# Half-width pairs for the first sixteen expert blocks of the output products

## The chip, the core and the metric

One core of a Trainium2 chip runs the whole kernel. It has five engines that run side by side: TensorE (matmuls, in the profile PE, and its weight loads, PEld), VectorE (DVE), ScalarE (ACT), GpSimd (POOL) and SyncE (SP), which issues most of the DMAs. TensorE reads two operands from the on-chip memory: a stationary one, which a weight load puts into the array of 128 rows and 128 columns, and a moving one, whose columns are streamed through it. It writes sums into eight accumulator banks of 128 partitions by 512 single-precision numbers.

The metric is device time in microseconds (us), the median of the runs.

## The reference

Input `x` has 2048 tokens of D = 576 numbers. Two results are mixed by a gate g, a sigmoid of a weighted sum of the token:

```
g = sigmoid((x * gate_w).sum(-1))
a = long convolution of x with a kernel K (a state space model), plus x * Dskip
b = expert layer:
    q = x @ w_q                  # 32 heads, two halves of 128 each
    s1, s2 = q1 @ k1.T, q2 @ k2.T    # 64 scores each
    the best two of s1 and of s2 give 4 candidates, the best two of them are kept
    weights = softmax of these two
    b = sum over heads and kept experts of  weight * gelu(x . u[e]) * v[e]
out = g * a + (1 - g) * b
```

There are 64 x 64 = 4096 experts, so `u` and `v` are 4096 x 576.

## The kernel before

The tokens are worked on in 16 tiles of 128. The kernel computes `x . u[e]` for all 4096 experts (tiles `a`), the scores (`s`), the convolution by matmuls with Fourier tables (`kb`, `kP`, `u`, `k`, `pr`, `pi`, `pv`, `y`), and then, tile by tile, a dense matrix of 128 tokens by 4096 experts that holds the weights at the kept experts and zeros elsewhere, multiplied by gelu of `x . u[e]`. The output stage multiplies this matrix with `v`.

For a token tile, the weighted matrix is made in `prep` (L1498): one-hot matrices `A`, `Bg` on VectorE, `S` on TensorE (L1528, four bursts of 32 matmuls, two banks each), the product with gelu (`gl`) on VectorE, and the split of the result into two 16-bit parts `wh` (L1558): `h[0]` the value rounded to 16 bits, `h[1]` what is left. Each has 32 blocks of 128 experts (partitions) by 128 tokens. `v` lies split in the same way in `vhl`, eight tiles of four blocks.

The output loop (L1775 to L1805) goes over the tiles in the order of `ORDER` (0, 15, 1, 14, ...). For each tile it takes two banks `po[0]` and `po[1]`, one for each half of D (288 columns). For each of the 32 blocks it issues three products (high by high, high by low, low by high) for both halves: six matmuls with the stationary operand `h[wz][:, b, :]` (128 experts by 128 tokens) and the moving operand 288 columns of `vhl`. A tile is 192 matmuls. The last tile in the order goes through one half of D after the other (L1793 to L1802), so that the first half can be finished while the second is summed up. `finish` (L1632) adds the result to `ya`, which holds the gated convolution from `y_part` (L1566), and sends it out.

What stands between these matmuls on TensorE is decided when the program is built. `mm` (L207) adds an estimated duration to a clock, and `pump` (L220) is called after each block and runs every waiting piece of work (a generator) that is due by that clock: a burst of `S` for the next tile, or the `y` matmuls of the next two tiles. `mm` also counts a change in the shape of the array's use with 0.13 or 0.1 us. The engines then run what was issued in that order, and wait only where data or a bank is not there yet.

Some matmuls use only a part of the array: `wb` (L593) and `tr` put 64 columns on each half of the array's columns, `kb` and `y` 32 columns on each quarter, `u` 64 rows on each half of the rows, `pr` and `pv` quadrants. Single-precision matmuls appear in the profile as two instructions each.

The helper `mm` records every matmul, so all of them have line L214; the tiles' names tell them apart.

Of the kernel before, what the change touches and what calls it, by code (L numbers as in the profile page):

```python
# [138 lines left out]
def body(ctx: ExitStack, tc: tile.TileContext, xT, au, par, logdt, dskip, gatew, wq, kT, uT, vv,  # L139
# [17 lines left out]
    def key(x):  # L157
        n = x.tensor.name
        return (n, x.offset) if n in columns else n

    def size(x):
        n = 1
        for d in x.shape[1:]:
            n *= d
        return n
# [41 lines left out]
    def mm(o, l, r, start, stop, cost=None):  # L207
        m = l.shape[0] > 64, 128 if size(l) > 64 else size(l)
        if m != tiling[0]:
            tiling[0] = m  # L210
            clock[0] += 0.13 if m == (True, 128) else 0.1
        clock[0] += (size(r) * (4 if r.dtype == F32 else 1) / 2400 + 0.003) if cost is None else cost
        rdy[key(o)] = clock[0] + 0.4
        T.matmul(o, l, r, start=start, stop=stop)  # L214

    def spawn(gen, after=0.0):
        heapq.heappush(heap, (clock[0] + after, nseq[0], gen))
        nseq[0] += 1

    def pump():  # L220
        while heap and heap[0][0] <= clock[0]:
            _, _, gen = heapq.heappop(heap)
            try:
                spawn(gen, next(gen) or 0.0)
            except StopIteration:
                pass
# [8 lines left out]
    def ready(*xs, late=0.0):  # L235
        while True:
            t = max(rdy.get(key(x), 0.0) for x in xs) + late - clock[0]
            if t <= 0:
                return
            yield t  # L240

    def wait(gen):
        for t in gen:
            idle(t)
# [16 lines left out]
    def need(tag, n=1):  # L261
        while True:
            lst = sorted(slots[tag])
            if len(lst) >= n and lst[n - 1] <= clock[0]:
                return
            yield max(0.2, lst[n - 1] - clock[0]) if len(lst) >= n else 0.3
# [6 lines left out]
    def free(tag, *outs):  # L273
        if owed[tag]:
            owed[tag] -= 1
            return
        slots[tag].append(max([clock[0]] + [rdy.get(key(x), 0.0) for x in outs]))
# [12 lines left out]
    def bank(tag, name):  # L290
        take(tag, name)
        t = ps.tile([128, 512], F32, tag="ps", name=name, bufs=8)
        banks.add(t.tensor.name)
        return t
# [1326 lines left out]
    def finish_half(t, po, hh):  # L1621
        yield from ready(po[hh])
        a = yt[t]
        half_rows(t, a, po, hh)
        yield from ready(a)
        cs = slice(288 * hh, 288 * hh + 288)
        for n, (d, o) in enumerate(au_rows(out, t, a)):
            dma(d[:, cs], o[:, cs], nc.scalar if hh and n % 2 else None)
        if hh:
            finished[t] = 1  # L1630

    def finish(t, po):  # L1632
        yield from ready(*po)
        while t not in yt:
            yield 0.3
        a = yt.pop(t)
        for hh in range(2):
            half_rows(t, a, po, hh)
        yield from ready(a)
        for d, o in au_rows(out, t, a):  # L1640
            dma(d, o)
        finished[t] = 1
# [54 lines left out]
    def until(f, dt=0.3):  # L1697
        while not f():
            idle(dt)
# [10 lines left out]
    for w, n in ((0, 9), (1, 5)):  # L1710
        for xk in [x for k in range(4) for x in (k, 4 + k)[:2 - w]] + [8]:
# [3 lines left out]
            for j in range(4):  # L1715
                cs = slice(128 * j, 128 * j + 128)
# [58 lines left out]
    for t in ORDER:  # L1775
        until(lambda: t in st)
        h = st.pop(t)
        wait(ready(*h))
        wait(need("sc", 2))
        po = [bank("sc", f"o{t}_{hh}") for hh in range(2)]  # L1780
        for b in range(32):
            if t == ORDER[0] and b % 4 == 0:
                until(lambda: len(vhl) > b // 4)
                wait(ready(vhl[b // 4]))
            if t == ORDER[-1]:
                break
            vc = vhl[b // 4]
            for n, (wz, vz) in enumerate(((0, 0), (0, 1), (1, 0))):
                for hh in range(2):
                    mm(po[hh][:, :288], h[wz][:, b, :], vc[:, b % 4, vz, 288 * hh:288 * hh + 288],  # L1790
                       b == 0 and n == 0, b == 31 and n == 2)
            pump()
        if t == ORDER[-1]:  # L1793
            until(lambda: t in yt)
            for hh in range(2):
                for b in range(32):
                    for n, (wz, vz) in enumerate(((0, 0), (0, 1), (1, 0))):
                        mm(po[hh][:, :288], h[wz][:, b, :], vhl[b // 4][:, b % 4, vz, 288 * hh:288 * hh + 288],
                           b == 0 and n == 0, b == 31 and n == 2)
                    pump()  # L1800
                spawn(finish_half(t, po, hh))
            break  # L1802
        free("slot")
        free("slot")
        spawn(finish(t, po))  # L1805
# [42 lines left out]
```

## Time and profile before

| what | value |
|---|---|
| median of three runs | 1449.73 us (1449.56 to 1449.82) |
| span of the profiled execution | 1447.6 us |
| `o` matmuls, busy, count | 387.0 us, 3072 |
| `s` and `a` matmuls, busy | 363.9 and 359.7 us, 1536 each |
| `S` matmuls, busy, count | 72.3 us, 2048 |
| `y` matmuls, busy, count | 17.2 us, 256 |
| weight loads of `wh`, busy, count | 296.0 us, 3072 |
| output stage on TensorE, first to last `o` start | 995.8 to 1443.7 us |

The span is the time from the first to the last instruction of one profiled execution. Busy time of an engine is the time in which at least one of its instructions runs; the ends of matmuls are modelled, so one `o` matmul is shown with 286 ns though another starts before it has ended. Durations below are therefore taken from start to start. A row of the timeline has the start, the time up to the last end of the row, the engine, the operation with output and inputs, the shapes, and the number of instructions.

### The profile page before, as it was taken

What the parts mean: (1) busy time and instruction counts of PE and PEld (TensorE: products, weight loads), DVE (VectorE), ACT (ScalarE), POOL (GpSimd) and SP (SyncE); (2) the same over time, 40 slices, a digit from 0 to 9 for tenths busy, and PEclk for the clock granted to TensorE, in tenths of its full rate; (3) what the DMA queues carried; (4) which work ended last, traced back from release to release, by engine and by line L of the source; (5) the groups of instructions that cost most, each with busy time, mean ns of one, the idle gap of its engine ahead of it and who ended that gap; (6) DMA issues with size and microseconds to landing.
All of it is one profiled execution on the core that took longest, in us unless ns stands there. A gap on an engine that the chain in (4) does not pass through costs nothing.

```text
span 1447.6 us, 36680 instructions
## 1 busy us (share of the span) xinstructions
PE 1426.9 (99%) x14105; PEld 852.3 (59%) x14105; DVE 1208.5 (83%) x4598; ACT 769.6 (53%) x1285; POOL 481.5 (33%) x491
## 2 busy tenths in 40 slices
PE   7999999999999999999999999999999999999998
PEld 3444445455455445445555444456887887888787
DVE  6899899889877997885899897589999988888850
ACT  6346876796684776844656655655434223323310
POOL 0325357547356436220547899600000000000000
PEclk9999999999999999999999999999999999999999
DMA  8235323342324333169675777776543333342400
GB/s 308 74 117 159 96 74 120 125 143 72 117 93 150 95 105 99 49 199 293 209 272 179 255 256 270 267 259 210 196 127 111 108 120 107 123 145 68 157 10 17
DMA packets 134351, 215.42 MB, mean 149 GB/s; under 512 B 10912, under 2 KB 79904, under 8 KB 127776
## 3 DMA queue, kind: packets, MB, share of 16 engines
q1 hardware_dynamic: 134080, 213.01, 45.5%
q8 instruction: 110, 1.80, 0.5%
q14 instruction: 65, 0.53, 0.1%
q10 hardware_dynamic: 96, 0.07, 0.0%
HBM read 141.74 MB, written 71.30 MB: 147 GB/s over the span
## 4 chain that ended last, share of the span: by engine, by line
PE 89%; DMA 2%; DVE 2%; issue 0%; ACT 0%; SPq 0%; ACTq 0%; DVEq 0%
PE o L214 26%; PE s L214 24%; PE a L214 23%; PE S L214 4%; PE kb L214 2%; PE pr L214 2%; PE wb L214 2%; PE y L214 1%; PE kP L214 1%; PE pv L214 1%; PE u L214 1%; PE k L214 1%; DMA z_d<-vo 1%; DMA ksb<-k_d 1%; DVE i L134 1%; DMA vn<-in_au_dram 0%
## 5 line engine op out<-in xcount | busy, mean ns | idle before, releaser
L214 PE MATMUL o<-vhl,wh 128*128 128x288 f16 x3072 | 387.0, 286 | 0.0
L214 PE MATMUL s<-whl,xb 128*128 128x512 f16 x1536 | 363.9, 379 | 0.0
L214 PE MATMUL a<-xb,uhl 128*128 128x512 f16 x1536 | 359.7, 379 | 0.2 <-DVE go L134 0.2
L214 PEld LDWEIGHTS <-wh 128*128 128x128 f16 x3072 | 296.0, 98 | 76.3 <-issue 3.7
L214 PEld LDWEIGHTS <-xb 128*128 128x128 f16 x1792 | 170.6, 98 | 210.1 <-issue 15.3
L214 PEld LDWEIGHTS <-uhl 128*128 128x128 f16 x1536 | 147.3, 98 | 176.2 <-issue 3.4
L134 DVE FIND_INDEX8 i<-m,s 128x8 uint32<-128x64 f32 x1024 | 206.5, 222 | 0.0
L134 ACT ACTIVATE wh<-gl,s_wg 128x1024 f16<-128x1024 f32 x64 | 68.9, 1137 | 202.3 <-DVE gl L134 202.3
L134 DVE MAX8 m<-s 128x8 f32<-128x64 f32 x1024 | 146.3, 215 | 29.3 <-PE s L214 28.4
L134 POOL TENSOR_TENSOR CS<-CS,ex 128x512 f32<-128x512 f32 x72 | 98.0, 1393 | 147.6 <-DVE ex L134 146.2
L134 ACT ACTIVATE go<-a,i_a 128x512 f32<-128x512 f32 x94 | 63.2, 685 | 96.4 <-PE a L214 68.6
L134 DVE TENSOR_TENSOR gl<-S,gl 128x256 f32<-128x256 f32 x256 | 90.5, 416 | 12.6 <-PE S L214 8.3
L134 POOL TENSOR_TENSOR e<-aN,rt 128x512 f32<-128x512 f32 x72 | 83.2, 1177 | 49.9 <-PE kb L214 43.7
L134 DVE SCALAR_TENSOR_TENSOR wh<-gl,s_wg,wh 128x1024 f16<-128x1024 f32 x63 | 78.6, 1280 | 10.7 <-ACT wh L134 10.7
L134 DVE TENSOR_TENSOR Bg<-Be,vals 128x1024 f16<-128x1024 f16 x128 | 84.6, 702 | 2.2
L134 ACT ACTIVATE gl<-gl 128x1024 f32<-128x1024 f32 x64 | 63.5, 1045 | 34.2 <-DMA gl<-g_d 31.1
L134 DVE TENSOR_TENSOR A<-iota_a,vals 128x2048 f16<-128x2048 f16 x64 | 77.9, 1216 | 0.0
L214 PE MATMUL s<-wrem,xb 128*128 128x512 f16 x256 | 76.2, 379 | 0.0
L214 PE MATMUL a<-xb,wrem 128*128 128x512 f16 x256 | 75.9, 379 | 0.0
L214 PEld LDWEIGHTS <-A 128*128 128x128 f16 x2048 | 70.5, 97 | 4.7
L134 DVE MATCH_VALUE_LOAD i<-m,s 128x8 f32 x1024 | 72.6, 71 | 0.1
L214 PE MATMUL S<-Bg,A 128*128 128x64 f16 x2048 | 72.3, 193 | 0.0
(205 smaller groups left out, 2068.5 us busy)
## 6 DMA issues: line engine op xcount, KB each, us to landing
g_d<-go SPq DMA_DIRECT2D x128, 256.0 KB, 2.5
gl<-g_d SPq DMA_DIRECT2D x32, 1024.0 KB, 5.4
wq<-in_wq_dram SPq DMA_DIRECT2D x16, 1152.0 KB, 6.0
su_d<-us SPq DMA_DIRECT2D x32, 288.0 KB, 2.6
sk_d<-k1o SPq DMA_DIRECT2D x32, 288.0 KB, 2.9
ui<-su_d SPq DMA_DIRECT2D x16, 576.0 KB, 4.0
ki<-sk_d SPq DMA_DIRECT2D x16, 576.0 KB, 5.3
vn<-in_vv_dram SPq DMA_DIRECT2D x32, 288.0 KB, 5.4
```

The source lines that it names most:

```text
L134: return f(*a, **k)
L214: T.matmul(o, l, r, start=start, stop=stop)
```

## The change

In the output loop, for all tiles but the last of the order, the blocks 0 to 15 are computed with half the tokens at a time. For each of the six former matmuls there are two: the tokens 0 to 63 (m = 0) on the array's first 64 columns and the tokens 64 to 127 (m = 1) on its last 64. The two that follow one another work on different halves of D, and so on different banks and different moving operands: with `hh = 0`, m = 0 goes to `po[0]` and m = 1 to `po[1]`; with `hh = 1` the other way round. Over both values of `hh` each quarter of the output (64 tokens by 288 columns) gets the same three products as before. The first product of block 0 opens the sum in each of the four quarters; the blocks 16 to 31 go on adding in the full shape. The planner's duration of one such matmul is given as 0.061 us.

```diff
             for n, (wz, vz) in enumerate(((0, 0), (0, 1), (1, 0))):
                 for hh in range(2):
+                    if b < 16:
+                        for m in range(2):
+                            cs = slice(64 * m, 64 * m + 64)
+                            z = 288 * (hh ^ m)
+                            mm(po[hh ^ m][cs, :288], h[wz][:, b, cs], vc[:, b % 4, vz, z:z + 288],
+                               b == 0 and n == 0, False, 0.061)
+                        continue
                     mm(po[hh][:, :288], h[wz][:, b, :], vc[:, b % 4, vz, 288 * hh:288 * hh + 288],
-                       b == 0 and n == 0, b == 31 and n == 2)
+                       False, b == 31 and n == 2)
             pump()
```

## The prediction

> **What bounds the kernel now.** I read the head of the page first, then the chain that ended last, then the output stage alone.
>
> ```profile
> span 1447.6 us, 36680 instructions
> ...
> PE 1426.9 (99%) x14105; PEld 852.3 (59%) x14105; DVE 1208.5 (83%) x4598; ACT 769.6 (53%) x1285; POOL 481.5 (33%) x491
> ...
> PEclk9999999999999999999999999999999999999999
> ...
> PE 89%; DMA 2%; DVE 2%; issue 0%; ACT 0%; SPq 0%; ACTq 0%; DVEq 0%
> PE o L214 26%; PE s L214 24%; PE a L214 23%; PE S L214 4%; PE kb L214 2%; PE pr L214 2%; PE wb L214 2%; PE y L214 1%; PE kP L214 1%; PE pv L214 1%; PE u L214 1%; PE k L214 1%; DMA z_d<-vo 1%; DMA ksb<-k_d 1%; DVE i L134 1%; DMA vn<-in_au_dram 0%
> ```
>
> TensorE is busy 99% of the span at full granted clock, and 89% of the chain is its work; the largest piece, 26%, is `o`, the products that the change rewrites. A busy TensorE need not be at its peak, so the next views are of the output stage: busy time of each engine in 50 us of it, then who waited for whom from 1000 us on (total us, times, longest).
>
> ```profile
> 1150.00:1200.00 50.00, 50.00 (x608) 41.18 (x610) 42.87 (x74) 15.10 (x15) 0.00 (x0) 1.00 0.39 124
> ```
>
> ```profile
> DVE ya L134 <- PE o L214: 58.0, 14, 20.2
> ...
> DVE gl L134 <- PE S L214: 7.7, 9, 1.6
> ...
> PEld L214 <- issue: 3.7, 8, 0.5
> ```
>
> The columns are PE, PEld, DVE, ACT, POOL, granted clock, DMA share and GB/s. TensorE has no idle time. VectorE is busy 42.87 of 50 us and waits for TensorE (58.0 and 7.7 us), not the other way round; the weight loads never wait longer than 0.5 us. So a nanosecond added to TensorE here is a nanosecond added to the end, and there is no wait in which it could vanish.
>
> The timeline of TensorE over one output tile and its neighbours (start us, us to the modelled end, what, how many) gives the rates, from start to start:
>
> ```profile
> 1163.01 15.60 PE L214 MATMUL o<-vhl,wh 128*128 128x288 f16 x126
> 1178.45 1.13 PE L214 MATMUL S<-Bg,A 128*128 128x64 f16 x32
> 1179.42 0.90 PE L214 MATMUL o<-vhl,wh 128*128 128x288 f16 x6
> 1180.15 1.13 PE L214 MATMUL S<-Bg,A 128*128 128x64 f16 x32
> 1181.12 4.57 PE L214 MATMUL o<-vhl,wh 128*128 128x288 f16 x36
> 1185.53 1.13 PE L214 MATMUL S<-Bg,A 128*128 128x64 f16 x32
> 1186.50 3.84 PE L214 MATMUL o<-vhl,wh 128*128 128x288 f16 x30
> 1190.17 1.13 PE L214 MATMUL S<-Bg,A 128*128 128x64 f16 x32
> 1191.14 8.25 PE L214 MATMUL o<-vhl,wh 128*128 128x288 f16 x66
> 1199.32 2.15 PE L214 MATMUL y<-yz,tf 128*32 128x288 f32 x32
> 1201.40 0.30 PE L214 MATMUL o<-vhl,wh 128*128 128x288 f16 x1
> ```
>
> 126 `o` take 1178.45 - 1163.01 = 15.44 us, 122.5 ns each. The bursts of `S`, 32 matmuls in 0.97 us, cost nothing extra at their edges: 30 `o` from 1186.50 to 1190.17 are 3.67 us, 122.3 ns each. Before `y`, which runs in another shape (four groups of 32 columns), it is different: 66 x 0.1225 = 8.09 us, but `y` starts after 8.18, so 0.09 us are lost at the change of shape.
>
> **The change part by part.** *Removed:* in 15 tiles, 16 blocks x 3 products x 2 halves of D = 96 full matmuls each, 1440 in all. *Added:* 2880 matmuls of 64 tokens, in 1440 pairs, with 2880 weight loads of 64 columns in place of 1440 of 128. Nothing else is moved by hand: same operands, same banks, same end of each sum, no DMA and no wait added. Each pair streams 288 columns on both halves of the array, so the question is what a pair costs, and what the added changes of shape cost.
>
> *The pair.* No row shows a 16-bit pair of 288 columns on two column halves. The nearest rows: `u`, 16-bit pairs on two row halves; `y` above, four column groups with four different moving operands; and the 64-column loads and matmuls of `tr`.
>
> ```profile
> 97.69 0.91 PE L214 MATMUL u<-uh,tu 64*128 64x288 f16 x12
> 98.54 0.60 PE L214 MATMUL s<-wrem,xb 128*128 128x512 f16 x2
> ...
> 933.82 0.20 PEld L214 LDWEIGHTS <-vals 128*64 128x64 bf16 x4
> ...
> 933.88 0.26 PE L214 MATMUL tr<-identb,vals 128*64 128x64 bf16 x4
> ```
>
> 12 `u` take 98.54 - 97.69 = 0.85 us, 6 pairs of 0.126 after 0.09 for the change of shape: two row halves run side by side at the price of one full matmul. For `y`, from the first start to the last (2.15 less the 0.41 of one matmul) seven groups of four take 1.74 us, 0.249 a group, or 0.124 for every two matmuls of 288 columns, with four operands read at once in a wider type. So two halves of the array reading two operands are not beyond the reading side. If four column groups run two by two, or as one at half speed, a pair of `o` comes out at 0.1225 either way. Bounds: 0.1225 (no row of 288 columns is shorter) and the 0.126 of `u`, 1440 x 3.5 ns = 5.0 us. I take 0.1225, a pair at the price of the full matmul, since both rows still hold a first load that nothing hides.
>
> *The loads.* A `tr` load of 64 columns starts 0.06 us before its first matmul (933.82 to 933.88): that is what it costs where nothing hides it. Within a run of pairs it lies beside 0.1225 us of the pair before, as 0.059 a pair does even where the matmuls are short (`wb`, below). Cost 0; if that cover were gone, 1440 x 0.06 = 86 us, but `wb` and `y` show loads and matmuls of the same groups overlapped. The Trainium skill, "TensorEngine Tiling (Array Packing)", section "Feature Incompatibilities", speaks against the change: column tiling is mutually exclusive with the fast weight load; by its "TensorE: Matmul & The Clock Gate", section "LDWEIGHTS (loading the stationary operand)", 64 columns then take 64/1.2 = 53 ns, an estimate. The trace agrees (0.06 us), and by the page the sum would be the same, since 53 ns is shorter than a pair.
>
> *The issue.* Four instructions in 122.5 ns instead of two. In `kb` the engine takes them faster:
>
> ```profile
> 164.89 0.32 PE L214 MATMUL kb<-Y,CS 128*32 128x64 f32 x8
> ...
> 166.59 0.29 PE L214 MATMUL kb<-e,CS 128*32 128x64 f32 x8
> ```
>
> 16 such rows of 8, from 164.89 to 166.88 (the last start plus its 0.29), are 128 matmuls in under 2 us, 16 ns each with its load, where the change asks for one in 61. Cost 0.
>
> *The change of shape.* `wb` has the very shape of the change, 128 rows by 64 columns:
>
> ```profile
> 24.27 0.81 PE L214 MATMUL a<-xb,uhl 128*128 128x512 f16 x3
> 25.01 2.32 PE L214 MATMUL wb<-kt,wq 128*64 128x64 f32 x72
> 27.26 2.76 PE L214 MATMUL a<-xb,uhl 128*128 128x512 f16 x12
> 29.86 0.38 PE L214 MATMUL a<-xb,wrem 128*128 128x512 f16 x1
> ```
>
> An `a` takes (29.86 - 27.26)/12 = 0.217 us, three 0.65, and `wb` starts after 0.74: 0.09 to drain on the way in, as before `y`. 72 `wb` last 2.25 us to the next `a`; from first to last start they take 2.32 - 0.22 = 2.10, 0.059 for each of 36 pairs, 2.11 in all: 0.14 us remain, of which 0.05 is the first load that nothing hides and 0.09 to 0.10 the drain on the way out. With 0.02 for the first full load and the skew of the last pair (an estimate: the rows are read to 0.01), one visit to the half-column shape costs 0.255 us. Bounds: 0.19 (two drains of 0.095, loads hidden) and 0.30 (a load of 0.06 exposed on both sides).
>
> *How many visits.* Each of 15 tiles enters the shape at block 0 and leaves it after block 15: 15 visits. `S` stays in the full shape, so each burst of `S` inside the first sixteen blocks adds one. I cut the 15 stretches of 96 `o` out of the trace and counted the `S` in each (us, PE busy and count, DVE, clock, DMA):
>
> ```profile
> 1023.45:1039.27 15.82, 2.26 (x64) 3.78 (x11) 1.00 0.44 153
> 1053.99:1066.66 12.67, 1.13 (x32) 2.83 (x8) 1.00 0.55 161
> 1082.35:1097.19 14.84, 1.13 (x32) 1.82 (x6) 1.00 0.09 22
> 1111.92:1125.55 13.63, 2.26 (x64) 1.41 (x4) 1.00 0.82 254
> ...
> 1367.15:1382.97 15.82, 2.26 (x64) 1.41 (x4) 1.00 0.27 86
> 1396.72:1408.42 11.70, 0.00 (x0) 0.00 (x0) 1.00 0.11 25
> ```
>
> Ten stretches in a row, 1111.92 to 1382.97, have 64 (two bursts); before them 64, 32, 32; the first and the last stretch none. A burst is 32, so 20 + 4 = 24. `y` lies inside seven first halves; it changes the shape on both sides before and after, so it adds no visit, only the exposed 64-column load on the way back, 7 x 0.04 = 0.3 us. In the first tile `y` stands where block 15 ends and saves half a visit, 0.13.
>
> *The sum.* (15 + 24) x 0.255 = 9.9, + 0.3 - 0.1 = 10.1 us, all of it on TensorE and on the path. The span goes from 1447.6 to 1457.7; the median lies 2.1 us above the span (1449.73 - 1447.6), so **1459.8 us**, 0.7% slower. The cost model of the planner counts a change of shape with 0.1 and 0.13, so later `S` bursts move back against the blocks by a block or so; the two in a first half stand at blocks 12 to 14, those of the second half from 19 on, and only in the third and fourth tile do some stand at 16 to 18. I allow 22 to 30 bursts. What waits behind a drain is only the next matmul; VectorE gets its `S` later by at most one drain and has 7 of 50 us to spare. The last tile (237 `o` from 1414.74, no change of shape) is not touched.
>
> ```profile
> 1414.74 29.20 PE L214 MATMUL o<-vhl,wh 128*128 128x288 f16 x237
> ```
>
> **Rivals.** *A, the pair costs a few ns more than a full matmul* (its two starts are not hidden): 1.44 us for each ns; at 7 ns 1459.8 + 10.1 = 1470. Against it: `u` at 0.126 with its first load in it. 13%.
>
> *B, the change does not do what it says: the halves run only partly side by side, or one after the other.* One after the other, 1440 x 0.1225 = 176 us more: 1636. Against it: 32 `y` of 288 columns take 2.08 us, where 32 x 0.1225 = 3.92 would be the least in series. Partly: if four fifths of the overlap come, a pair takes 0.1225/0.79 = 0.155, 47 us more: 1507. The Trainium skill, "TensorE: Matmul & The Clock Gate", section "Measured speedup vs the span model", has three column tiles at 2.38 times one, which is this 0.79; the trace speaks against it, as groups of `y` come at twice 0.124. 3% together.
>
> *C, not slower: a pair streams faster than a full matmul.* Place: the 1440 pairs; each ns under 122.5 gives 1.44 us back, and at 122.5 - 10.1/1.44 = 115.5 ns the drains are paid for: 1449.7. Below that the kernel would be faster. For it: nothing in a run of `o` shows whether the last 2 ns are the array or the hand-over between matmuls; against it: no row of 288 columns comes under 0.122. 3%, of which 1% is faster.
>
> *D, the order of the bursts shifts.* If none of the `S` fell into a first half, 24 visits fewer: 1459.8 - 6.1 = 1453.7; if all four did in 14 tiles, 71 visits, 32 more: 1468.0. 8%, mostly between.
>
> **How the numbers follow.** Forecast 73%, its own bounds 37 x 0.19 = 7.0 and 45 x 0.30 = 13.5, so 1456.7 to 1463.2. For 8 in 10 I add the nearer part of A (up to 5 ns, 7.2 us: 1467) and of D: **1455.5 to 1467**. A measurement can tell about 0.2%, 2.9 us, from no change: for that fewer than 12 visits would have to be paid, and the tiles alone make 15. Faster 1%, within 0.2% 2%, slower 97%.
>
> **What would show it.** In the profile after: pairs of `o` with 64 columns at 122.5 ns from pair to pair (A and B: longer, C: shorter); 0.09 us lost before and after each run of them, and a first pair about 0.05 late; 22 to 30 bursts of `S` inside first halves; still no idle TensorE and the same granted clock; other stages unchanged. I am wrong if TensorE's gaps at the edges are under 0.05 us, if pairs are not at 122.5, or if a weight load becomes what the matmuls wait for.

## The result and the profile after

| | before | after |
|---|---|---|
| median, us | 1449.82 (1449.56 to 1452.7, 5 runs) | 1460.03 (1456.4 to 1460.77, 5 runs) |
| span of the profiled execution, us | 1447.6 | 1458.8 |
| first to last start of an output matmul, us | 447.9 | 456.8 |

The ratio is 1.0061, with a 95% interval of 1.0043 to 1.0078: slower by 0.6%, at 1460.0 us where 1459.8 was forecast, in the range of 1455.5 to 1467. Two more sets of runs say the same: 1.0064 (1.0047 to 1.0081) for the changed kernel again, 1.0004 (0.9993 to 1.0016) for the kernel before against itself.

The last row of the table is read from these two, before and after: count, then shortest, median and longest duration in ns, then the first and the last start in us (the counts behind the shapes are of a sample). With one more digit of the trace the differences are 1443.65 - 995.77 = 447.9 and 1454.89 - 998.09 = 456.8.

```profile
L214 PE MATMUL o<-vhl,wh x3072: 283/286/297, 995.8 to 1443.7; 128*128 128x288 f16 x192
```

```profile
L214 PE MATMUL o<-vhl,wh x4512: 283/286/310, 998.1 to 1454.9; 128*64 128x288 f16 x124, 128*128 128x288 f16 x73
```

The head of the page after:

```profile
span 1458.8 us, 39560 instructions
...
PE 1436.8 (98%) x15545; PEld 871.6 (60%) x15545; DVE 1210.2 (83%) x4598; ACT 770.2 (53%) x1285; POOL 481.5 (33%) x491
```

1440 more matmuls and as many loads, as counted, and about 10 us more of TensorE's time. VectorE has the same instructions as before. Whether TensorE waits now is read from the view of who waited for whom, from 998 us on:

```profile
DVE ya L134 <- PE o L214: 62.8, 15, 20.4
...
PEld L214 <- issue: 14.2, 54, 0.5
DVE gl L134 <- PE S L214: 11.2, 9, 1.8
```

The order of who waits has not changed: VectorE for TensorE, a little longer than before (58.0 and 7.7 us then). The one row that grew for TensorE is the weight loads' (3.7 us in 8 waits, now 14.2 in 54): by their places in the trace, the 8 are the returns from `y`, and the 46 new ones all stand at a change into or out of the half-column shape.

Where the time lies shows in the timeline of TensorE, here over the paired blocks of one tile. `128*128` is the full shape, `128*64` the half columns; two of the latter are a pair. The row of `o` between the first two that are shown is left out, as it holds matmuls of both shapes, and the last row ends where the view does.

```profile
1138.07 1.13 PE L214 MATMUL S<-Bg,A 128*128 128x64 f16 x32
...
1147.33 2.15 PE L214 MATMUL y<-yz,tf 128*32 128x288 f32 x32
1149.41 6.07 PE L214 MATMUL o<-vhl,wh 128*64 128x288 f16 x96
1155.41 1.14 PE L214 MATMUL S<-Bg,A 128*128 128x64 f16 x32
1156.48 1.66 PE L214 MATMUL o<-vhl,wh 128*64 128x288 f16 x24
1158.07 1.14 PE L214 MATMUL S<-Bg,A 128*128 128x64 f16 x32
1159.14 1.05 PE L214 MATMUL o<-vhl,wh 128*64 128x288 f16 x14
```

A "drain" is here, as in the prediction, the time lost between the last matmul of one shape and the first of another; what TensorE does in it, no run shows. 96 half matmuls, 48 pairs, take 1155.41 - 1149.41 = 6.00 us; 48 x 0.1225 is 5.88, and 0.12 remain for one late first pair and one drain. 24 of them take 1.59 us, 12 x 0.1225 = 1.47 and again 0.12. And a burst of `S` that stood free of cost among full matmuls (0.97 us) now takes 1.07 us to the next pair (1155.41 to 1156.48): the other drain, 0.10. So the time is at the edges, 0.22 us for each visit to the half-column shape, and none in the pairs.

Taken over all starts of the stage, pairs follow one another every 122 or 123 ns (1346 intervals, without the first of each run of pairs), as full matmuls do, and the terms of a visit are these: into the shape 0.092 to 0.093 us, a first pair of 0.1465 instead of 0.1225 (0.024), out of it 0.099, and about 0.01 for the first full matmul after it, 0.224 together. There are 40 visits, 15 for the tiles and 25 for bursts of `S`: 9.0 us, of 456.8 - 447.9 = 8.9.

### The profile page after: what moved, and what is told of

It is laid out like the page before. It is cut to its first block, busy times and chain, and to the rows that moved or that the text cites. A ratio compares the mean times of both kernels' runs of the same rounds, so it can differ in the third digit from the quotient of the medians.

```text
span 1458.8 us, 39560 instructions
## 1 busy us (share of the span) xinstructions
PE 1436.8 (98%) x15545; PEld 871.6 (60%) x15545; DVE 1210.2 (83%) x4598; ACT 770.2 (53%) x1285; POOL 481.5 (33%) x491
## 4 chain that ended last, share of the span: by engine, by line
PE 89%; DMA 2%; DVE 2%; issue 0%; SPq 0%; ACT 0%; DVEq 0%; ACTq 0%
PE o L214 26%; PE s L214 23%; PE a L214 22%; PE S L214 4%; PE kb L214 2%; PE pr L214 2%; PE wb L214 2%; PE y L214 1%; PE kP L214 1%; PE pv L214 1%; PE u L214 1%; PE k L214 1%; DMA wq<-in_wq_dram 1%; DMA ksb<-k_d 1%; DVE i L134 1%; DMA gw<-in_gatew_dram 0%
## 5 line engine op out<-in xcount | busy, mean ns | idle before, releaser
L214 PE MATMUL o<-vhl,wh 128*64 128x288 f16 (+1 forms) x4512 | 391.0, 287 | 0.0
L214 PEld LDWEIGHTS <-wh 128*64 128x64 f16 (+1 forms) x4512 | 315.5, 105 | 61.9 <-issue 10.0
```

## The experiments

Two theories stood against each other. V: each visit to the half-column shape costs 0.224 us and a pair costs nothing more than a full matmul. P: the pairs cost the 8.9 us, 6.2 ns each. V's 0.224 was read from the changed kernel, so what tests it is whether it holds for other numbers of visits and pairs. The output stage alone is compared, from the first to the last start of an `o`, since what lies ahead of it scatters by some us from run to run (last section). The first row behind each expectation is that of the `o` matmuls, as above; other rows show waits: who waited for whom, total us, times, longest.

**More visits, the same pairs.**

```diff
-                    if b < 16:
+                    if b % 2 == 0:
```

> The same 1440 pairs, but in the even blocks of all 32: 234 visits. Theory V: 447.9 + 234 x 0.224 = 500.3 us for the output stage. Rival P: 456.8 us.

```profile
L214 PE MATMUL o<-vhl,wh x4512: 283/286/310, 997.9 to 1499.4; 128*64 128x288 f16 x125, 128*128 128x288 f16 x72
```

1499.4 - 997.9 = 501.5 us, 53.6 more than before, 0.229 for each of the 234 visits and 1.2 us above V's number. The median is 1503.6 us, ratio 1.0364 (1.0336 to 1.0392). P, at 456.8, falls: the number of pairs is the same as with the change.

**More pairs, some more visits.**

```diff
-                    if b < 16:
+                    if b < 32:
-                               b == 0 and n == 0, False, 0.061)
+                               b == 0 and n == 0, b == 31 and n == 2, 0.061)
```

> Pairs in all 32 blocks of the fifteen tiles: 2880 pairs, 57 visits. Theory V: 447.9 + 57 x 0.224 = 460.7 us for the output stage. Rival P: 447.9 + 2880 x 6.2 ns = 465.7 us.

```profile
L214 PE MATMUL o<-vhl,wh x5952: 286/286/310, 994.2 to 1456.6; 128*64 128x288 f16 x192, 128*128 128x288 f16 x7
```

```profile
PEld y L214 <- DMA yz<-z_d: 1.6, 1, 1.6
```

462.4 us, of which 1.6 are one wait of a `y` load for its operand from memory: 460.8 without it, as V says. Twice the pairs, and the price follows the visits. Ratio 1.0092 (1.0062 to 1.0122).

**Few pairs, fifteen visits.**

```diff
-                    if b < 16:
+                    if b < 1:
```

> Pairs only in block 0 of the fifteen tiles: 90 pairs, 15 visits. Theory V: 447.9 + 15 x 0.224 = 451.3 us for the output stage, the same as with 1440 pairs in 15 visits. Rival P: 447.9 + 90 x 6.2 ns = 448.5 us.

```profile
L214 PE MATMUL o<-vhl,wh x3162: 283/286/310, 993.5 to 1446.6; 128*128 128x288 f16 x187, 128*64 128x288 f16 x11
```

```profile
PE S L214 <- DVE Bg L134: 1.6, 2, 1.2
```

453.1 us: more than either theory. 1.6 us are two waits of `S` for its one-hot matrices, which the view of before does not have; without them 451.5, near the 451.3 of V and 3 us from P. Why they come here was not looked into. The median is 1455.9 us, ratio 1.0039 (1.0027 to 1.005): 90 pairs bring more than half of the slowdown that 1440 bring; in the stage of this execution, without the waits, it is 3.6 of 8.9 us, near the share of their visits (15 of 40).

**All pairs, fifteen visits.** This was to give the price of the pairs alone.

```diff
-            pump()
+            if b >= 15:
+                pump()
```

> All 1440 pairs stay, but the planner lets other work in only after block 15, so no S burst splits the paired blocks: 15 visits to the half-column shape instead of 40. Theory V (each visit costs 0.224 us, a pair costs what a full matmul costs): from the first to the last start of an output matmul 447.9 + 15 x 0.224 = 451.3 us. Rival P (the pairs cost it, 8.9 us / 1440 = 6.2 ns each): 456.8 us as with the change. More than either if the later S bursts starve what follows; then TensorE would show idle time.

```profile
L214 PE MATMUL o<-vhl,wh x4512: 283/286/449, 998.0 to 1482.1; 128*64 128x288 f16 x124, 128*128 128x288 f16 x73
```

```profile
PE S L214 <- DVE Bg L134: 19.9, 15, 6.7
PEld L214 <- DVE Bg L134: 18.6, 9, 6.8
...
PE S L214 <- DVE ya L134: 1.5, 1, 1.5
PE o L214 <- DVE ya L134: 0.9, 1, 0.9
```

484.1 us, ratio 1.0254 (1.0222 to 1.0286): both numbers missed, and the third case of the expectation came. The bursts that were held back then stood close together, each of them needs work of VectorE that can begin only after an earlier one, and TensorE waited 19.9 us for it. The longest `o` of 449 ns belongs to what followed: after such waits the granted clock was 0.50 for some us (0.992 on average over the span). So the total of the stage says nothing on the pairs. Their starts do: 1374 of the 1425 intervals from pair to pair are 122 or 123 ns, and the others stand at the start of a run or in such a stretch of low clock. The run also says what letting the bursts into the paired blocks is worth: saving their 25 visits, 5.6 us, cost 33 us of another kind.

**One operand for both halves.**

```diff
-                            z = 288 * (hh ^ m)
-                            mm(po[hh ^ m][cs, :288], h[wz][:, b, cs], vc[:, b % 4, vz, z:z + 288],
+                            z = 288 * hh
+                            mm(po[hh][cs, :288], h[wz][:, b, cs], vc[:, b % 4, vz, z:z + 288],
```

> As the change, but the two halves of a pair take the same half of D: the same 288 moving columns and the same bank. 40 visits. Theory V: 456.8 us for the output stage, no difference. Rival (two different moving operands, or two banks, cost something): less than 456.8. Rival (both halves writing one bank get in each other's way): more, by 1.44 us for each ns a pair gets longer.

```profile
L214 PE MATMUL o<-vhl,wh x4512: 283/286/310, 997.0 to 1453.7; 128*64 128x288 f16 x124, 128*128 128x288 f16 x73
```

456.7 us, as V says: the crossing of the halves of D costs and brings nothing, nor does one bank for both halves. Ratio 1.0063 (1.0043 to 1.0082).

**Both kernels once more.**

> The changed kernel once more. The output stage takes 456.8 us again. The stages before it, 2.3 us longer in the first profile (998.1 us to the first output matmul instead of 995.8), hold none of the change: if that was chance, the first output matmul starts anywhere between 995 and 999 us, and the median of the ratio comes nearer to 1.0062 (8.9 us); if the program's greater length makes it, 998 again.

> The kernel before once more, for a second profile of it: output stage 447.9 us; if the start of the stage scatters by chance, its first matmul is not at 995.8 us again.

```profile
L214 PE MATMUL o<-vhl,wh x4512: 283/286/310, 996.7 to 1453.5; 128*64 128x288 f16 x124, 128*128 128x288 f16 x73
```

```profile
L214 PE MATMUL o<-vhl,wh x3072: 283/286/297, 995.1 to 1443.1; 128*128 128x288 f16 x192
```

The stage is 456.8 us for the change and 448.0 for the kernel before, again: it repeats to 0.1 us, and 8.8 us lie between them (456.75 less 447.99 with one more digit). The first `o` starts at 996.7 us where it was 998.1, and at 995.1 where it was 995.8, so the start scatters within one kernel; the ratio of 1.0064 is no nearer to 1.0062 than the first, 1.0061.

**The halves one after the other.** Do the halves overlap because they are neighbours in the order?

Against the kernel before (the diffs above are against the changed one):

```diff
+            if b < 16:
+                for m in range(2):
+                    cs = slice(64 * m, 64 * m + 64)
+                    for n, (wz, vz) in enumerate(((0, 0), (0, 1), (1, 0))):
+                        for hh in range(2):
+                            mm(po[hh][cs, :288], h[wz][:, b, cs], vc[:, b % 4, vz, 288 * hh:288 * hh + 288],
+                               b == 0 and n == 0, False, 0.102)
+                pump()
+                continue
...
-                       b == 0 and n == 0, b == 31 and n == 2)
+                       False, b == 31 and n == 2)
```

> The same 2880 half matmuls, but in each block the six of tokens 0 to 63 first, then the six of tokens 64 to 127, so that neighbours stand on the same half of the array except at two places of a block; 68 visits. If two halves run side by side only when neighbours in the order, twelve take ten turns of 122.5 ns instead of six: 240 blocks x 4 x 0.1225 = 117.6 us and 15.2 for the visits, 580.7 us for the output stage. If the halves were served out of order: 463 us. If pairs never ran side by side at all, this kernel would take what the change takes, 456.8 and the longer way of the visits.

```profile
L214 PE MATMUL o<-vhl,wh x4512: 285/286/448, 1002.3 to 1501.1; 128*64 128x288 f16 x124, 128*128 128x288 f16 x73
```

498.8 us in the one execution that there is, none of the three numbers. The timeline of TensorE shows why:

```profile
1269.87 1.14 PE L214 MATMUL S<-Bg,A 128*128 128x64 f16 x32
1270.94 1.20 PE L214 MATMUL o<-vhl,wh 128*64 128x288 f16 x12
1272.07 1.14 PE L214 MATMUL S<-Bg,A 128*128 128x64 f16 x32
1273.14 3.40 PE L214 MATMUL o<-vhl,wh 128*64 128x288 f16 x48
1276.47 1.14 PE L214 MATMUL S<-Bg,A 128*128 128x64 f16 x32
```

Twelve half matmuls take 1272.07 - 1270.94 = 1.13 us; without 0.12 for the edges that is 8 turns of 0.1225 (a turn is the time of one pair, or of one half matmul alone), where in order it would be 11. 48 take 3.33 us: 26 turns, 24 for pairs and 2. In the trace a run begins with two that start alone and ends with two alone, and in between two start in every 122.5 ns. So matmuls of the second half run beside those of the first that stand several places ahead of them. The rest of the 50.9 us: 68 visits 15.2; two turns in each of 76 runs (the 8 that follow a `y` are among them) 18.6; some 17 are left, among them waits for the operands of `S` and `y` and stretches at a lower granted clock, not taken apart further.

**Twelve of one half first.** If the engine looks ahead, how far?

Against the run above, with the lines between left out:

```diff
             if b < 16:
+                if b % 2 == 0:
+                    continue
                 for m in range(2):
                     cs = slice(64 * m, 64 * m + 64)
+                    for c in (b - 1, b):
...
-                            mm(po[hh][cs, :288], h[wz][:, b, cs], vc[:, b % 4, vz, 288 * hh:288 * hh + 288],
-                               b == 0 and n == 0, False, 0.102)
+                                mm(po[hh][cs, :288], h[wz][:, c, cs], vc[:, c % 4, vz, 288 * hh:288 * hh + 288],
+                                   c == 0 and n == 0, False, 0.11)
```

> As e4_one_half_first, but over two blocks: twelve half matmuls of tokens 0 to 63, then twelve of tokens 64 to 127; 54 visits and 62 runs of half matmuls. In e4 two half matmuls started in every 122.5 ns all the same, and at the head of a run two started alone. Theory Q (a matmul for the free half overtakes those that wait for the other half, from at most some four places further back): a run starts with eight alone instead of two, then goes on in pairs: 447.9 + 54 x 0.224 + 62 x 8 x 0.1225 = 520.8 us for the output stage, and some 5 to 15 us of waits for late S operands. Rival in order (only neighbours run side by side): ten turns more for 24 matmuls, 120 x 10 x 0.1225 = 147 us, 607. Rival without a limit: two alone at most, 475 and the waits.

```profile
L214 PE MATMUL o<-vhl,wh x4512: 283/286/445, 997.7 to 1556.5; 128*64 128x288 f16 x124, 128*128 128x288 f16 x73
```

```profile
1273.06 1.14 PE L214 MATMUL S<-Bg,A 128*128 128x64 f16 x32
1274.12 2.67 PE L214 MATMUL o<-vhl,wh 128*64 128x288 f16 x24
1276.72 1.14 PE L214 MATMUL S<-Bg,A 128*128 128x64 f16 x32
```

24 take 2.60 us, less 0.12 for the edges 2.48, or 20 turns: between 12 (all in pairs) and 23 (only neighbours). The starts in the trace are eight alone, four pairs, eight alone. The head is as theory Q says, eight alone, since the ninth is four places ahead of the thirteenth; but "then in pairs" was wrong, as after four pairs the first half has nothing left within reach. The stage took 558.8 us in its one execution, not 520.8. The whole stage fits a reach of four places: counted from the starts, 1456 half matmuls run alone and 712 pairs side by side, as four places give for these runs. That is 728 turns more than all in pairs, 89 us; with 12 us of visits the stage would be 549, and 10 us (low clock and waits among them) are not taken apart. So a matmul for the free half is taken from at most four places behind the one that runs. Which half a start belongs to isn't recorded; that is concluded from the rate: the eight alone come one in 122.5 ns, so two starts within a turn are taken to be on two halves.

No run points to a version faster than the kernel before: a full matmul takes 122.5 ns for 288 columns and 128 tokens, and no pair in any of these runs takes less for the same work.

## Why the prediction was right

- *TensorE is the bound and no wait hides anything.* Right: the stage grew by 8.9 us, the sum of the visits (9.0) to 0.1 us.
- *A pair costs a full matmul, 0.1225 us.* Right, and shown: the rows of 96 and 24 half matmuls, and 2880 pairs in `e3_all_blocks` at the price of the visits. With rival A at 7 ns the stage would have been 10 us longer. B and C fall with the same rows.
- *Loads and issue cost nothing within a run.* Right; the new waits of loads are all at edges. The 0.06 us of `tr` was read in the middle of a run, though; at its head, the one place with nothing to hide a load, load and matmul start together in the records (933.58). The price of a first load is better read from how late the second pair comes, as below. Only the upper bound of a visit, 0.30 us, took the 0.06.
- *39 visits, 22 to 30 bursts.* Right: 40 visits, 25 bursts. From the fifth tile on the planner kept them at blocks 12 to 14, as before; one more, in the fourth tile, moved from 16 to 15. Rival D did not come.
- *0.255 us for a visit.* The mechanism right, the size a little off: the drains were 0.092 and 0.099, as read from `wb` and `y`, but the first load that nothing hides was put at 0.05 and showed as 0.024, and the 0.02 of the estimate as about 0.01. The 0.05 was read rightly: the first pair of `wb`, with single-precision operands, takes 0.106 us where the later ones take 0.058. It did not carry over to the 16-bit pairs; why, no run shows. The returns from `y` came to about 0.01 each, not 0.04. This is why the stage's forecast was 10.1 us instead of 8.9.
- *The total, 1459.8 against 1460.0.* Closer than the terms deserve, and that is luck: the stage grew by 1.2 us less than forecast, and the part before it, which the prediction took as unchanged, was longer, by 2.3 us in the profiled execution (998.1 less 995.8). What it was in the executions without a profile isn't known. The interval of the ratio, 6.2 to 11.3 us, holds both 8.9 and 10.1.

(The matmuls of `wb` stand in line 585 of the kernel before, not in 593.)

## What to carry to other kernels

In this kernel (16 bits, 288 columns), splitting a matmul that already fills the array into two halves gained nothing and lost some 0.22 us each time the stream of matmuls went into the smaller shape and came back; price such a change by its visits, counting all that the order puts in between, not by its matmuls. If a partial shape is needed, gather the work of that shape; but holding back the other work for that cost six times what it saved here, because the bursts then stood so close together that TensorE waited for VectorE between them. And compare stages, start to start: these repeat to 0.1 us where whole runs of one kernel scatter by several us.

## What was not expected of the hardware

As far as the rate shows it, TensorE does not start matmuls strictly in order when they use different column halves. With six of one half ahead of six of the other, two started in every 122.5 ns but for two alone at each end of a run; with twelve and twelve, only four pairs came for each change of half. Both fit a reach of four places.

The part before the output stage scatters. Over eleven profiled executions the first `o` started between 993.5 and 1002.3 us, though the instructions ahead of it are the same in all of them. One place of it shows in the timelines of before and after:

```profile
456.23 0.25 PE L214 MATMUL kb<-e,CS 128*32 128x64 f32 x3 [1.50 <-issue]
```

```profile
457.57 0.25 PE L214 MATMUL kb<-e,CS 128*32 128x64 f32 x3 [2.60 <-issue]
```

```profile
458.00:460.00 2.00, 2.00 (x14) 0.73 (x8) 0.69 (x1) 1.66 (x2) 1.64 (x2) 0.50 0.03 8
```

In the middle of a run of `kb` TensorE stands still with nothing to wait for in the profile, 1.50 us before and 2.60 after, and after the longer one the granted clock is 0.50 for a while (the 0.50 behind the busy times in the last row, a view of 2 us of the changed kernel). In the six other executions with as many matmuls as the changed kernel (one is its own second profile) this gap was 1.77 to 3.00 us, in the second profile of before 1.47, and in the programs with 2880 and with 90 pairs 1.23 and 1.15. Whether something in the program sets it, or chance, stays open; no run was made for it.
